# A transformer-like chain on one core: the second MLP's token blocks taken in pairs with Strassen's seven products

## The chip, the cores and the metric

The kernel runs on one core of a Trainium2 chip. The metric is device time of one execution in microseconds (us); lower is better. Engines are named as the profile names them: PE is TensorE (its weight load PEld stands apart), DVE VectorE, ACT ScalarE, POOL GpSimd, SP the queue from which most DMAs are issued.

## The reference

Everything is float32 but the weights, which are float64 (two 32-bit words for each element).

```
attention, per batch and head, 576 tokens x 64:   q' = softmax over features of q, k' = softmax over tokens of k
                                                  x  = q' @ (k'^T @ v)
x reshaped to 4608 tokens x 512 features
first MLP:   h = x @ w_in (512 x 2048);  g = h * clip(h + 3, 0, 6) / 6;  x = g @ w_out (2048 x 512)
second MLP:  h = x @ w_in2;              g = h * sigmoid(h);             out = g @ w_out2
```

## The kernel before

The 4608 tokens are nine blocks of 512 (`BLK`), the 2048 hidden features sixteen tiles of 128 (`NF`). One step is one block and one hidden tile; there are 9 x 16 steps of the first MLP, then 9 x 16 of the second. Every matmul operand is split in two fp32r parts, a rounded upper one and the remainder as lower one, and each product is three matmuls (upper x upper, upper x lower, lower x upper). So a step has 12 matmuls of the first layer (`mm1`, L430: four tiles of 128 input features x 3, 512 tokens as the moving columns) and 12 of the second (`mm2`, L500 and L502). Between them stands the gate (L461 and above): ScalarE's activation, VectorE's product, ScalarE's cast to the upper part, VectorE's subtraction for the lower part. In the first MLP `mm2` leaves its sum with features on partitions, written to `yd` in DRAM (`finish`, L512); in the second one the gate's result is the stationary operand, so the sum has tokens on partitions and is stored as it is.

The order of all instructions on every engine is the order in which the code writes them. The first block is ordered by a small planner (`Plan`); everything after it by the loop at L829. In each step of this loop stand the steps of the attention (a unit is two heads of one block; it takes seven steps, of which `begin` gives the first): among them `k_max` (L227 to L229) at the end of a unit's first step, and in the next one the PE transpose `k_turn` (L234), after `mm1`. In every fourth step of the loop (those with number 1 modulo 4) the next unit's first step meets the older unit's fifth, with the kv scaling `kv_upper` (L291).

The second MLP's weights come as float64. `Conv` turns a tile of 128 x 512 into the two fp32r parts: `begin` (two ScalarE operations), `bits` (three VectorE operations), `upper` (a ScalarE cast), `lower` (a VectorE subtraction). During blocks 1 to 7 of the first MLP, 32 conversions are done, each within one step, and stored to `wd` in DRAM from the single buffer "sp" (L157); the raw tiles are loaded by `load_w`. In the first MLP's last block the converted weights come back with `load_split` into the 16 "wi" and 16 "wo" tiles, where they stay for the second MLP. Its input blocks are read back with `load_y` and split with `split_y`.

PSUM has eight banks of 512 columns: two "h", two "a", four "y0" to "y3". The pools of SBUF that the change uses again are `wts` (16 "wi" and 16 "wo" tiles of 4 KB a partition), `xs` (two of 16 KB), `raw`, `tmp` (six of 2 KB), `gs` and `att`.

## Time and profile before

| what | value |
|---|---|
| three timed runs | 1704.63, 1705.07, 1707.39 us (median 1705.07) |
| profiled execution, first to last instruction (its span) | 1703.8 us |
| its own time around the span | not listed; the median of the timed runs is 1.3 us above the span |
| mean granted clock of TensorE | 0.999 of full speed |
| PE, DVE, ACT, POOL busy | 1669.1, 782.8, 613.6, 77.0 us |
| moved by DMA | 139.22 MB |

The span is that of one execution under the profiler. Busy time counts an engine's instructions, not its waits. Matmuls overlap one another in the list, so the path's cost of one is read from the distance of their starts.

### The profile page before, as it was taken

What the parts mean: (1) busy time and instruction counts of PE and PEld (TensorE: products, weight loads), DVE (VectorE), ACT (ScalarE), POOL (GpSimd) and SP (SyncE); (2) the same over time, 40 slices, a digit from 0 to 9 for tenths busy, and PEclk for the clock granted to TensorE, in tenths of its full rate; (3) what the DMA queues carried; (4) which work ended last, traced back from release to release, by engine and by line L of the source; (5) the groups of instructions that cost most, each with busy time, mean ns of one, the idle gap of its engine ahead of it and who ended that gap; (6) DMA issues with size and microseconds to landing.
All of it is one profiled execution on the core that took longest, in us unless ns stands there. A gap on an engine that the chain in (4) does not pass through costs nothing.

```text
span 1703.8 us, 20315 instructions
## 1 busy us (share of the span) xinstructions
PE 1669.1 (98%) x7868; PEld 1362.7 (80%) x7868; DVE 782.8 (46%) x1424; ACT 613.6 (36%) x1073; POOL 77.0 (5%) x82
## 2 busy tenths in 40 slices
PE   6999999999999999999999999999999999999998
PEld 4777887888788877888888888888888888888887
DVE  8997555565656555555323232223332223332322
ACT  6885344443444344434222222222222222222222
POOL 2110000000000000000000000000000000000000
PEclk9999999999999999999999999999999999999999
DMA  8912443443444335232464010101010101000000
GB/s 259 318 38 83 109 123 105 114 133 108 121 115 133 106 97 139 81 106 62 143 209 153 9 38 13 37 13 38 13 37 13 37 13 36 14 31 20 21 5 25
DMA packets 169808, 139.22 MB, mean 82 GB/s; under 512 B 105840, under 2 KB 140656, under 8 KB 169712
## 3 DMA queue, kind: packets, MB, share of 16 engines
q1 hardware_dynamic: 106752, 122.68, 23.2%
q10 hardware_dynamic: 62960, 15.25, 4.0%
q8 instruction: 62, 1.02, 0.3%
q14 instruction: 34, 0.28, 0.0%
HBM read 95.16 MB, written 42.73 MB: 81 GB/s over the span
## 4 chain that ended last, share of the span: by engine, by line
PE 86%; DVE 7%; ACT 2%; DMA 2%; issue 1%; ACTq 1%; POOL 0%; DVEq 0%; POOLq 0%
PE h L430 41%; PE y L502 23%; PE y L500 18%; PE pa L388 1%; ACTq L361 1%; DVE fa L127 1%; DVE fa L131 1%; PE pa L274 1%; DVE r L450 1%; DMA zd<-qz 1%; DMA qt<-zd 1%; ACT g L458 1%; DVE fa L120 0%; ACT r L443 0%; ACT fa L114 0%
## 5 line engine op out<-in xcount | busy, mean ns | idle before, releaser
L430 PE MATMUL h<-x,wi 128*128 128x512 f32 x3456 | 841.4, 391 | 2.4 <-DVE wi L154 1.0
L430 PEld LDWEIGHTS h<-x,wi 128*128 128x128 f32 x3456 | 644.8, 188 | 139.3 <-DVE wi L154 2.9
L500 PE MATMUL y<-g,wo 128*128 128x512 f32 x1728 | 420.7, 392 | 0.0
L502 PE MATMUL y<-wo,g 128*128 128x512 f32 x1716 | 412.2, 389 | 0.0
L502 PEld LDWEIGHTS y<-wo,g 128*128 128x128 f32 x1716 | 322.1, 188 | 66.9
L500 PEld LDWEIGHTS y<-g,wo 128*128 128x128 f32 x1728 | 320.9, 188 | 68.2 <-ACT g L458 0.4
L454 DVE TENSOR_TENSOR r<-r,h 128x512 f32<-128x512 f32 x144 | 99.0, 688 | 455.5 <-ACT r L445 455.5
L445 ACT ACTIVATE r<-h 128x512 f32<-128x512 f32 x144 | 86.1, 598 | 468.8 <-PE h L430 468.8
L461 DVE TENSOR_TENSOR g<-r,g 128x512 fp32r<-128x512 f32 x272 | 188.4, 693 | 141.6 <-ACT g L458 129.8
L458 ACT CAST g<-r 128x512 fp32r<-128x512 f32 x272 | 169.0, 621 | 222.6 <-DVE r L450 114.0
L450 DVE SCALAR_TENSOR_TENSOR r<-r,h 128x512 f32<-128x512 f32 x128 | 87.8, 686 | 242.2 <-ACT r L443 241.8
L443 ACT ACTIVATE r<-h 128x512 f32<-128x512 f32 x144 | 86.2, 598 | 165.1 <-PE h L430 154.3
L335 POOL TENSOR_TENSOR qe<-qe,qs 128x512 f32<-128x512 f32 x36 | 37.6, 1045 | 355.7 <-DVE qs L330 351.6
L291 ACT ACTIVATE kv<-pa,rs 64x64 fp32r<-64x64 f32 x56 | 17.3, 309 | 98.9 <-DMA qt<-zd 38.5
L313 POOL TENSOR_TENSOR qe<-qraw,qm 128x512 f32<-128x512 f32 x34 | 35.9, 1056 | 365.4 <-DVE qm L305 278.0
L127 DVE CUSTOM_DVE_ANT_0 fa<-fa,fr 128x1024 uint16<-128x1024 uint16 x64 | 46.3, 723 | 7.6 <-ACT fr L116 0.5
L120 DVE TENSOR_SCALAR fa<-fa 128x512 uint32<-128x512 uint32 x64 | 30.0, 468 | 39.0 <-ACT fa L114 38.8
L388 PE MATMUL pa<-qT,kv 128*128 128x512 f32 (+7 forms) x192 | 38.3, 329 | 1.1 <-DVE qT L373 1.1
L264 ACT ACTIVATE ke<-ke 128x640 f32<-128x640 f32 x32 | 23.7, 739 | 40.3 <-DVE ke L254 40.3
L388 PEld LDWEIGHTS pa<-qT,kv 128*128 128x128 f32 x192 | 31.2, 196 | 6.4 <-DVE qT L373 3.2
L398 ACT CAST x<-pa 128x512 fp32r<-128x512 f32 x36 | 21.1, 585 | 29.0 <-PE pa L388 28.9
L274 PEld LDWEIGHTS pa<-vbuf,ke 128*64 128x64 f32 (+1 forms) x560 | 20.8, 136 | 11.7 <-issue 6.7
(96 smaller groups left out, 716.8 us busy)
## 6 DMA issues: line engine op xcount, KB each, us to landing
wd<-sp SPq DMA_DIRECT2D x32, 512.0 KB, 3.0
yd<-o SPq DMA_DIRECT2D x36, 256.0 KB, 2.8
yr<-yd SPq DMA_DIRECT2D x36, 256.0 KB, 2.7
wi_early<-in_moe_w_in_dram SPq DMA_DIRECT2D x16, 512.0 KB, 9.3
wo_early<-in_moe_w_out_dram SPq DMA_DIRECT2D x16, 512.0 KB, 9.5
wi_raw<-in_moe_w_in_dram SPq DMA_DIRECT2D x16, 512.0 KB, 4.9
wo_raw<-in_moe_w_out_dram SPq DMA_DIRECT2D x16, 512.0 KB, 4.7
wi<-wd SPq DMA_DIRECT2D x16, 512.0 KB, 3.6
```

Of the source, the lines that this page charges most:

```text
L127: nc.vector.tensor_tensor(out=au, in0=au, in1=self.r, op=ALU.add)
L274: nc.tensor.matmul(pk[d, 0 : D + 1], t[0:n, j, d], tv[0:n, j, h, :], start=(j == 0), stop=(j == KCH),)
L388: nc.tensor.matmul(pv[:, :, p0 : p0 + n], w[:, a, :], qT[:, c, :, p0 : p0 + n], start=(n_ == 0 and p0 == 0), stop=(n_ == 2), skip_group_ch ...
L430: nc.tensor.matmul(h, w[:, a, c, :], x[:, e, c, :], start=(c == 0 and n == 0), stop=(c == NC - 1 and n == 2),)
L443: nc.scalar.activation(self.r, self.h, AF.Relu, bias=3.0)
L445: nc.scalar.activation(self.r, self.h, AF.Sigmoid)
L450: nc.vector.scalar_tensor_tensor(out=r, in0=r, scalar=6.0, in1=h, op0=ALU.min, op1=ALU.mult)
L454: nc.vector.tensor_tensor(out=r, in0=r, in1=h, op=ALU.mult)
L458: nc.scalar.copy(self.g[:, 0], self.r)
L461: nc.vector.tensor_tensor(out=self.g[:, 1], in0=self.r, in1=f32(self.g[:, 0]), op=ALU.subtract)
L500: nc.tensor.matmul(y[c], w[:, a, cs], g[:, e, :], start=st, stop=sp)
L502: nc.tensor.matmul(y[c], g[:, e, cs], w[:, a, :], start=st, stop=sp)
```

## The change

The second MLP's first eight blocks to be worked on (1 to 8) are taken as four pairs; block 0 follows at the end as before. For a pair (j, j+1), a layer is one product of 2 x 2 blocks: the weights' blocks are `A11`, `A12`, `A21`, `A22` (halves of the inputs by neighbouring hidden tiles in the first layer, with a slot of 256 columns), the tokens' blocks `B11`, `B21` of block j and `B12`, `B22` of block j+1. Seven products replace eight:

```
weights' sums   S1 = A21 + A22   S2 = S1 - A11   S3 = A11 - A21   S4 = A12 - S2
tokens' sums    T1 = B12 - B11   T2 = B22 - T1   T3 = B22 - B12   T4 = B21 - T2
products        P1 = A11 B11   P2 = A12 B21   P3 = S4 B22   P4 = A22 T4   P5 = S1 T1   P6 = S2 T2   P7 = S3 T3
```

Both layers of a pair are done one after the other: for each of eight pairs of hidden tiles (`NPR` = 8) seven `inner` units of 6 matmuls each with the gate of its four results, then 7 x 8 `outer` units of 6 matmuls, product by product. An `outer` unit takes its token operand from `split` (ScalarE cast) and `split_low` (VectorE subtraction), up to three units ahead, through four buffers. The weights' parts lie in DRAM (`ws`, 128 parts of 256 KB, four halves and three sums for each pair of tiles and layer, and the fourth half alone) and are streamed by `fetch`, two parts of 256 KB at a time, through a ring of six buffers, anew for every pair of blocks. The sums of the second layer's products are gathered in eight SBUF rows (`fixed`), transposed in `turn` by PE, and stored.

In the first MLP, blocks 1 to 8, the conversions go by `Parts`: two tiles at once over seven steps (steps 1 to 7 and 8 to 14 of a block): `convert` of one and of the other, `sums` on GpSimd, and four steps with a cast, a subtraction and two stores each. In the first MLP's last block `first_operands` makes the first pair's token operands.

Core of the diff ("..." where lines are left out):

```diff
-    wd = dram.tile([NF, 2, P, 2, DM], F32, name="wd")
+    ws = dram.tile([2, 4 * NF, P, DM], F32, name="ws")
...
+    class Parts:
...
+        def convert(self, n):
+            self.conv[n].begin()
+            self.conv[n].bits()
+        def sums(self):
...
+            self.s = raw.tile([P, 4, HALF], F32, tag="raw", name="ws_sum")
...
+            for to, x, y, op in (
+                ("S1", "A21", "A22", ALU.add), ("S2", "S1", "A11", ALU.subtract),
+                ("S3", "A11", "A21", ALU.subtract), ("S4", "A12", "S2", ALU.subtract),
+            ):
+                nc.gpsimd.tensor_tensor(out=at[to], in0=at[x], in1=at[y], op=op)
+        def upper(self, n):
...
+            self.t = att.tile([P, 2, DM], F32R, tag="sp", bufs=1, name="sp")
+            nc.scalar.copy(self.t[:, 0], self.src)
+        def lower(self, n):
+            t = self.t
+            nc.vector.tensor_tensor(out=t[:, 1], in0=self.src, in1=f32(t[:, 0]), op=ALU.subtract)
+            for h, name in enumerate(self.names[n]):
+                nc.sync.dma_start(
+                    ws[self.o, slot(self.o, self.i, name)].rearrange("p (a d) -> p a d", a=2),
+                    f32(t)[:, :, h * HALF : (h + 1) * HALF],
+                )
...
+    def fetch(k):
+        o, m = divmod(k % (7 * NPR), 7 * NPR // 2)
+        nc.sync.dma_start(
+            f32(ring[k % len(ring)]),
+            ws[o, 2 * m : 2 * m + 2].rearrange("s p d -> p s d"),
+        )
...
+    def raw_x(to, j, h):
+        nc.sync.dma_start(to, yd[j, 2 * h : 2 * h + 2].rearrange("c p n -> p c n"))
+    def x_split(name, src=None):
+        hi, lo = op[name]
+        if src is None:
+            src = f32(lo)
+        nc.scalar.copy(hi, src)
+        nc.vector.tensor_tensor(out=lo, in0=src, in1=f32(hi), op=ALU.subtract)
+    def x_sum(to, x, y, how):
+        nc.gpsimd.tensor_tensor(out=to, in0=x, in1=y, op=how)
+    def x_steps(j):
...
+            t3=lambda: x_sum(st1, low("B22"), st2, ALU.subtract),
+            t1=lambda: x_sum(st2, st2, low("B11"), ALU.subtract),
+            t2=lambda: x_sum(st1, st1, low("B11"), ALU.add),
+            t4=lambda: x_sum(st1, low("B21"), st1, ALU.subtract),
+            T3=lambda: x_split("T3", st1),
...
+    KEYS = ("P1", "P7", "P6", "P5", "P3", "P4", "P2")
...
+        def inner(b, n, p):
...
+            for c in range(2):
+                ws_ = w[:, :, c * P : (c + 1) * P]
+                for m, (a, e) in enumerate(((0, hi), (0, lo), (1, hi))):
+                    nc.tensor.matmul(
+                        to, ws_[:, a], e[:, c],
...
+        def pair_events(b, n, t):
...
+            when(e["P1"] + 0.1, s1)
+            when(e["P6"] + 0.1, u2)
+            when(e["P5"] + 0.1, s5)
+            when(e["P2"] + 0.1, lambda: sig(b, n, "A"))
+            when(e["P2"] + 0.7, lambda: mul(b, n, "A", 0, 0))
+            when(e["P7"] + 0.1, u3)
+            when(e["P7"] + 0.6, c22)
+            when(e["P7"] + 1.1, lambda: sig(b, n, "22"))
+            when(e["P3"] + 0.1, c12)
+            when(e["P7"] + 1.7, lambda: mul(b, n, "22", 1, 1))
...
+            when(e["P3"] + 1.9, t3)
+            when(e["P3"] + 2.0, t1)
+        def split(b, p, i, u):
+            if u % 4 < 2:
+                t = gs.tile([P, 2, BLK], F32R, tag="g", name="gsp")
+            else:
+                tag = "sp" if u % 4 == 2 else "qT"
+                t = att.tile([P, 2, BLK], F32R, tag=tag, bufs=1, name="gsp")
+            d["sp", b, p, i] = t
+            nc.scalar.copy(t[:, 0], source(p, i))
+        def split_low(b, p, i):
+            t = d["sp", b, p, i]
+            add(t[:, 1], source(p, i), f32(t[:, 0]), ALU.subtract)
+            if p == "P1":
+                g1 = g_of(2 * i)
+                add(g1[:, 0], op["spare"][:, i], g1[:, 0], ALU.add, nc.gpsimd)
+            if p == "P6":
+                g1 = g_of(2 * i)
+                add(g1[:, 0], g1[:, 0], g_of(2 * i + 1)[:, 0], ALU.subtract, nc.gpsimd)
+        def outer(b, p, i):
...
+            for m in range(2):
+                for k, (a, e) in enumerate(((0, 0), (0, 1), (1, 0))):
+                    nc.tensor.matmul(
+                        d[b, p][m], w[:, a, m * P : (m + 1) * P], t[:, e],
...
+        def join(b, p):
+            for m in range(2):
+                one, two, three, c22 = fixed[4 * m : 4 * m + 4]
+                if p == "P1":
+                    nc.scalar.copy(one, d[b, p][m])
+                if p == "P6":
+                    add(two, d[b, p][m], one)
+                    add(three, d[b, "P7"][m], two)
+                if p == "P5":
+                    add(c22, d[b, p][m], three)
+                    add(two, d[b, p][m], two)
...
+        def turn(j, k, bank=bank):
...
+                    nc.tensor.transpose(
+                        at[:, c * P : (c + 1) * P], x[:, i * P : (i + 1) * P], ident
+                    )
+            o = small("o2")
+            nc.scalar.copy(o, at)
...
+            nc.sync.dma_start(rows[i], o)
...
+            for u in range(7 * NPR):
+                p, i = KEYS[u // NPR], u % NPR
+                t = start[u]
+                when(t - LOOK + 0.2, lambda b=b, p=p, i=i, u=u: split(b, p, i, u))
+                when(t - LOOK + 0.5, lambda b=b, p=p, i=i: split_low(b, p, i))
+                when(t, lambda b=b, p=p, i=i: outer(b, p, i))
...
+                if i == NPR - 1:
+                    when(t + 1.3, lambda b=b, p=p: join(b, p))
+            j = 1 + 2 * b
+            if b + 1 < BB:
+                do = x_steps(j + 2)
+                base = start[0]
+                for x, name in (
+                    (3.1, "b22"), (3.2, "b11"), (3.3, "b21"), (14.3, "b12"), (17.5, "t3"),
+                    (19.6, "T3"), (19.7, "t1"), (22.6, "t2"), (23.6, "T1"), (26.6, "T2"),
+                    (28.6, "t4"), (31.6, "B11"), (34.6, "T4"), (37.6, "B21"), (40.6, "B22"),
+                ):
+                    when(base + x, do[name])
+                for k in range(2 * NCH):
+                    when(T + 3.95 + 5.0 * k, lambda j=j, k=k: turn(j, k))
+            else:
...
+                for f in range(NF):
+                    when(base + (4.2 + 2.2 * f if f < 14 else 100.0), lambda f=f: load_split(f, 0))
+                for f in range(0, NF, 2):
+                    when(base + 48.3 + 0.5 * f, lambda f=f: load_split(f, 1))
...
+                when(uses[k] + 1.0 - 0.01, lambda k=k: fetch(k + 6))
...
+        parts_at = {}
+        for n in range(2 * NPR):
+            for r in range(7):
+                parts_at[(n // 2 + 1) * NF + 1 + 7 * (n % 2) + r] = (n, r)
...
+        steps = [(0, j, f) for j in range(NB) for f in range(NF)]
```

Of the events of `pair_events`, `s1` and `s5` are ScalarE copies of P1 and P5; `u2`, `u3`, `c12` and `c21` are VectorE additions with one operand in PSUM; `c22` and the product of the same result (`mul` with "22") have both operands in SBUF; `sig` is ScalarE's sigmoid; `t3` and `t1` are GpSimd differences of gate results. Times in `when` are in units of one `inner` or `outer` call; the events are sorted by them and written in that order. Within a pair's second layer, unit u starts at base + u + 1 (from the second unit on).

## Rows read from the trace of the kernel before

**Rows 1.** The page: busy us, share of the span, instructions of each engine.

```profile
PE 1669.1 (98%) x7868; PEld 1362.7 (80%) x7868; DVE 782.8 (46%) x1424; ACT 613.6 (36%) x1073; POOL 77.0 (5%) x82
```

**Rows 2.** The page: chain that ended last, by engine and by line.

```profile
PE 86%; DVE 7%; ACT 2%; DMA 2%; issue 1%; ACTq 1%; POOL 0%; DVEq 0%; POOLq 0%
PE h L430 41%; PE y L502 23%; PE y L500 18%; PE pa L388 1%; ACTq L361 1%; DVE fa L127 1%; DVE fa L131 1%; PE pa L274 1%; DVE r L450 1%; DMA zd<-qz 1%; DMA qt<-zd 1%; ACT g L458 1%; DVE fa L120 0%; ACT r L443 0%; ACT fa L114 0%
```

**Rows 3.** Windows: us, busy PE PEld DVE ACT POOL, PEclk, DMA share, GB/s.

```profile
48.00:72.00 24.00, 23.89 (x121) 18.82 (x122) 23.24 (x46) 20.79 (x39) 2.25 (x2) 1.00 1.06 401
1050.00:1150.00 100.00, 100.00 (x443) 82.81 (x442) 29.05 (x43) 26.04 (x44) 0.00 (x0) 1.00 0.07 22
153.00:704.00 551.00, 542.06 (x2798) 440.39 (x2798) 327.49 (x655) 225.90 (x404) 46.98 (x45) 1.00 0.42 117
704.00:912.50 208.50, 208.29 (x936) 171.66 (x935) 89.00 (x148) 69.57 (x121) 9.39 (x9) 1.00 0.40 129
```

**Rows 4.** Timeline in the second MLP: start, us, engine, line, operation, count.

```profile
1301.71 2.88 PE L502 MATMUL y<-wo,g 128*128 128x512 f32 x12
...
1307.15 2.88 PE L502 MATMUL y<-wo,g 128*128 128x512 f32 x12
```

**Rows 5.** Timeline of PE around five transposes in the first MLP.

```profile
147.48 0.27 PE L246 MATMUL pa<-ident,mx 128*128 128x128 f32 x1
147.59 0.60 PE L343 MATMUL pa<-ident,qe 128*128 128x128 f32 x4
147.95 3.00 PE L430 MATMUL h<-x,wi 128*128 128x512 f32 x12
150.79 2.88 PE L500 MATMUL y<-g,wo 128*128 128x512 f32 x12
```

**Rows 6.** Groups by line: out<-in, shapes, count, busy us, mean ns, idle before.

```profile
L461 DVE TENSOR_TENSOR g<-r,g 128x512 fp32r<-128x512 f32 x272 | 188.4, 693 | 141.6 <-ACT g L458 129.8 <-PE y L502 5.5 <-PE y L500 1.4
L458 ACT CAST g<-r 128x512 fp32r<-128x512 f32 x272 | 169.0, 621 | 222.6 <-DVE r L450 114.0 <-DVE r L454 108.6
L335 POOL TENSOR_TENSOR qe<-qe,qs 128x512 f32<-128x512 f32 x36 | 37.6, 1045 | 355.7 <-DVE qs L330 351.6 <-ACT x L398 4.1
L254 DVE TENSOR_TENSOR ke<-kbuf,pa 128x640 f32<-128x640 f32 x28 | 22.8, 814 | 2.0 <-PE pa L246 2.0
```

**Rows 7.** PE's waits (sum, times, longest) from 153 us; timeline around two k_turns.

```profile
PE pa L234 <- DVE m L229: 8.2, 7, 1.4
...
254.14 0.63 ACT L291 ACTIVATE kv<-pa,rs 64x64 fp32r<-64x64 f32 x2 [2.89 <-DMA qt<-zd]
...
260.76 0.29 DVE L229 TENSOR_TENSOR m<-m,kbuf 128x128 f32<-128x128 f32 x1
261.19 0.30 PE L234 MATMUL pa<-ident,m 128*128 128x128 f32 x1 [1.37 <-DVE m L229]
...
305.83 0.63 ACT L291 ACTIVATE kv<-pa,rs 64x64 fp32r<-64x64 f32 x2 [4.00 <-PE h L430]
...
309.89 0.29 DVE L229 TENSOR_TENSOR m<-m,kbuf 128x128 f32<-128x128 f32 x1
310.58 0.27 PE L234 MATMUL pa<-ident,m 128*128 128x128 f32 x1
```

**Rows 8.** DMA issues: out<-in, queue, count, KB each, median us to landing.

```profile
wi<-wd SPq DMA_DIRECT2D x16, 512.0 KB, 3.6
```

**Rows 9.** Timeline of DVE and POOL where they meet, in the first block.

```profile
59.30 1.05 POOL L335 TENSOR_TENSOR qe<-qe,qs 128x512 f32<-128x512 f32 x1 [13.26 <-DVE qs L330]
59.36 0.69 DVE L467 SCALAR_TENSOR_TENSOR h<-r,h 128x512 f32<-128x512 f32 x1
...
60.82 0.68 DVE L154 TENSOR_TENSOR wo<-fa,wo 128x512 fp32r<-128x512 f32 x1
61.42 0.68 DVE L127 CUSTOM_DVE_ANT_0 fa<-fa,fr 128x1024 uint16<-128x1024 uint16 x1
61.79 1.21 POOL L313 TENSOR_TENSOR qe<-qraw,qm 128x512 f32<-128x512 f32 x1 [1.45 <-PE pa L343]
62.13 1.42 DVE L131 SCALAR_TENSOR_TENSOR fa<-wi_early,fa 128x512 uint32<-128x512 uint32 x1
```

More of the change, by code (lines that the diff above doesn't have):

```diff
@@ L880, in efficient_attention_then_two_mlps @@
                 q_norm(here[2], nc.gpsimd)
[L881 to L889 removed]
+            job, r = parts_at.get(n, (None, None))
+            if r in (0, 1):
+                made[job].convert(r)
+                if r == 1 and job + 1 < 2 * NPR:
+                    load_w(1, 2 * made[job + 1].i, made[job + 1].o)
+            if r == 2:
+                made[job].sums()
             mm1(s)
@@ L911, in efficient_attention_then_two_mlps @@
                 q_store(here[3])
-            for c in convs:
-                c.upper()
-                c.lower()
+            if r is not None and r >= 3:
+                made[job].upper(r - 3)
+                made[job].lower(r - 3)
             if 2 in has_k:
```

295 lines of the change are left out of this document (259 added, 36 removed), and 3 rows, old and new, of the table new.

## The prediction

> **What bounds the kernel now.** I read the page's busy shares first: TensorE works 98% of the 1703.8 us span, no other engine half of it [rows 1]. The chain of waits says the same of the path: 86% of it is TensorE, and its three largest parts are the two MLPs' matmuls [rows 2]. Then the stages: from 1050 to 1150 us TensorE is busy without a gap at granted clock 1.00, VectorE 29%, ScalarE 26%, GpSimd not at all, and the DMA engines move 22 GB/s; between 153 and 704 us, with the attention beside the first MLP, TensorE is idle 9 us in 551 and VectorE busy 59% [rows 3]. The timeline gives the second MLP's pace: from one second-layer group of 12 matmuls to the next is 1307.15 - 1301.71 = 5.44 us, and 24 matmuls lie in it, so one 128x512 matmul costs 0.2267 us on the path (its listed 0.39 us overlaps its neighbours) [rows 4]. In this stage only fewer matmuls shorten the time, as long as the rest keeps pace.
>
> **The change, part by part.** The sum starts from the profiled span, 1703.8 us; the median of the timed runs is 1705.07, so 1.3 us is added at the end.
>
> *Matmuls removed.* Two blocks of the second MLP are 2 x 16 steps x 24 = 768 matmuls. In the change a pair has 7 products x 8 indices x 6 matmuls = 336 per layer, 672 in all. Four pairs save 4 x 96 = 384, and 384 x 0.2267 = 87.0 us. The ninth block and the tail stay as they are.
>
> *Transposes added.* The second layer now leaves its sum with features on partitions, so each pair needs 8 turns of four 128x128 fp32 transposes, 128 in all. Between the matmuls of the first MLP five such transposes took: first issue 147.48, next group 147.95, and that group's 12 matmuls end 2.84 instead of 2.72 us later (150.79); 0.59 us for five, 0.118 each [rows 5]. 128 x 0.118 = 15.1 us on the path. Their evictions and stores lie on ScalarE and SP, beside.
>
> The Trainium skill, page "TensorE: Matmul & The Clock Gate", section "Part 4: PE-mode transpose", gives about 0.275 us for a 128x128 transpose inside a kernel and says that transposes do not count like matmuls for the clock. By that figure the term would be 35.2 us and the sum 20 us later; the rows time the same operation, at granted clock 1.00, so they are used.
>
> *First MLP.* 32 more casts (0.62 us) and 32 more subtractions (0.69 us) [rows 6] are 20 us of ScalarE and 22 us of VectorE over eight blocks, 64 half-width sums go to GpSimd, and 128 stores of 256 KB replace 32 of 512 KB. These engines have room [rows 3]. What counts is the one wait that TensorE has here: k_turn waits for the last k_max operation, 7 times, 8.2 us [rows 7]. It comes when a conversion falls in the step of k_max: without one, k_max ended 4.35 us after the kv scaling began (305.83 to 310.18) and TensorE did not wait; with a whole one it ended 6.91 us after (254.14 to 261.05) and TensorE waited 1.37 [rows 7]. So a conversion delays it 2.56 us, and some 1.2 of it is covered. Now the first half of a conversion (two ScalarE operations, three VectorE operations; the second half's 0.69 gone, so 1.9 us) falls into two of the four such steps of a block: 12 steps at 1.9 less a cover of 0.4 to 1.2 us are 8 to 18 us, against 8.2 now. I take a middle, 12, so +4 us; ends 0 and +20 (the upper one if the single "sp" buffer, whose store must land before the next cast, makes ScalarE wait as well, and with it all VectorE work queued behind the subtraction). The operands of the first pair are made in the last block, whose VectorE is 43% busy [rows 3]; nothing for it.
>
> *Weights from DRAM.* 56 fetches of 512 KB per pair, each for two units of 6 matmuls (2.72 us): 193 GB/s. Each waits on SP for the last matmul of its slot's old contents; behind it queue the next fetches, the raw x loads and the output stores. It is issued ten units, 13.6 us, before its use, and a 512 KB load lands in 3.6 us [rows 8]. The stage from 48 to 72 us moved 401 GB/s [rows 3]. In the last pair's second layer the ninth block's weights come beside it (14 x 512 KB in 41 us, 179 GB/s): 372, still below. Nothing on the path.
>
> *First layer of a pair.* Per index n (42 matmuls, 9.52 us): 9 VectorE operations, 6.2 us, 6 ScalarE, 3.6, two GpSimd, 2.1 [rows 6]. Each combination has three or more units before TensorE writes over its bank. Nothing, as estimate; the upper end is a rival.
>
> *Second layer of a pair.* Here each unit (1.36 us) needs a fresh split: a ScalarE cast and a VectorE subtraction of two SBUF operands. GpSimd adds 8 sums of 512 columns during P1, 8 during P6, and in the first three pairs four of 1024 columns (t1 to t4) for the next pair's x. What matters is whether GpSimd and VectorE can work at the same time. At 61.79 a GpSimd operation starts; the VectorE operation with two SBUF operands that starts at 62.13 takes 1.42 instead of 0.69 us and ends 0.55 after GpSimd's (63.55 to 63.00). A VectorE operation that reads PSUM, at 59.36 beside GpSimd's 59.30, is not delayed, and free VectorE operations follow each other every 0.60 us (60.82, 61.42) [rows 9]. So in these phases a sum (1.05) and a subtraction (0.60) go one after the other: 1.65 us per unit against TensorE's 1.36.
>
> The Trainium skill, page "SBUF — State Buffer", section "SBUF: two separate sides", says that the pair of ports shared by the two engines is held for a whole instruction and the other engine fully blocks. The rows agree for single meetings; with both queues full no run here shows it.
>
> A 1024-column split is 512's plus 512 columns at about 1.0 ns (640 columns 0.814, 512 0.693 [rows 6]): 1.2 us; a 1024-column sum, twice 1.05 less its start, 2.0. The three stretches of a full pair:
> - P1, from its second split to the eleventh unit: 10 subtractions 6.0, two first-layer operations with two SBUF operands 1.2, 9 sums 9.45, half of four PSUM-reading operations 1.3: 18.0 us, against 11.5 units, 15.6. About 2.0 late, less where they overlap better.
> - P6 to P5, 13 splits: 7.8; 8 sums 8.4; t3, t1, t2 6.0; splits T3 and T1 2.4; joining P6 with four VectorE operations 2.6: 27.2 us. TensorE takes 14.4 units, 19.6, counted from the earliest time that four split buffers allow. 7.6 late.
> - P5 with the B11 split and four joins before the backlog is gone: 1.0.
>
> That is 10.6 us for a full pair, three of them, 31.8. The last pair has no t sums, only four 512-column splits of y: 4 us. Together 36 us of new TensorE waits, whose releaser is the subtraction in split_low. Ends: 10 us if the ports do not exclude each other (joins and wide splits alone), 50 if GpSimd wins each tie, so that T1 and T2 come later still.
>
> **Sum.** 1703.8 - 87.0 + 15.1 + 4 + 36 = 1671.9, plus 1.3: **1673 us**.
>
> **Rivals.**
> - *The exclusion costs little.* VectorE and GpSimd interleave, or GpSimd falls behind harmlessly (the P6 sums are needed only in P4). For it: the first MLP's GpSimd work delays hardly anything. Against it: the meetings of [rows 9], and T1 waits in line behind those sums. Second-layer waits 10: 1673 - 26 = 1647 us.
> - *The first layer doesn't keep pace.* VectorE runs 9 operations per n in written order, four of them behind a ScalarE sigmoid; if each n adds 1 us of TensorE wait, 32 x 1 = 32: 1705 us, no change. Against it: 6.2 us of work in 9.5 and three units of lead. For it: today VectorE's chain has idle time in front of almost every operation.
> - *Slower: the weight stream sets the pace.* Break-even is a fetch period of 2.72 + (87.0 - 15.1 - 4)/224 = 3.02 us (173 GB/s) if nothing else waits. If one fetch must land before the next makes headway, its 3.6 us [rows 8] is the period: 224 x 0.88 = 197 us of waits, about 1705 - 68 + 197 = 1834. For it: 2 KB rows, one queue, all behind in-order waits. Against it: six buffers, and 401 GB/s with 512 KB loads in the same queue.
>
> **How the numbers follow.** Forecast 60%, little exclusion 22%, first layer 10%, stream 8%. Forecast's own spread with the first-MLP ends: 1652 to 1700. The range leaves out the stream, the upper half of the first-layer case and the lowest outcomes: 1640 to 1699. This kernel's runs tell 0.2%, 3.4 us, from no change. Faster: 60 + 22 + half of the first-layer case, with a little taken off for it: 87%; same 3%; slower 10%.
>
> **What would show it.** About 384 fewer 128x512 matmuls in the groups by line and 128 more transposes near 0.1 us apart. In the windows of a pair's second layer, TensorE idle 8 to 12 us of some 88, and in its waits the matmul of outer on VectorE's split_low subtraction, gathered at P6; almost none in the first layer. VectorE subtractions of 1.2 us and more beside GpSimd. In the first MLP k_turn's wait for k_max near 12 us. DMA near 200 GB/s in the second MLP, with no matmul waiting for it. The forecast is wrong if the waits are spread evenly over both layers, if a DMA is their releaser, or if TensorE runs without a gap in P6.

## The result, and the profile after

The changed kernel took 1725.15 us (median of 4 runs, 1723.13 to 1726.64) against 1704.99: a ratio of 1.0116 [1.0101, 1.0130], slower by 20 us. The forecast was 1673 us, its range 1640 to 1699, with a chance of 10% for slower. All times that follow are against the kernel before on the same chip.

The page of the changed kernel, busy time and chain, in the columns of [rows 1, 2]:

```profile
span 1721.3 us, 21607 instructions
PE 1631.2 (95%) x7612; PEld 1312.2 (76%) x7612; DVE 1080.8 (63%) x1748; ACT 741.7 (43%) x1285; POOL 357.4 (21%) x290
PE 70%; DVE 17%; ACT 4%; DMA 4%; issue 2%; POOL 1%; ACTq 1%; SPq 0%; DVEq 0%; POOLq 0%
```

TensorE has 256 instructions fewer (384 matmuls less, 128 transposes more, as forecast), but it falls from 98 to 95% busy, and VectorE's share of the chain rises from 7 to 17%. Where the time is lost shows in two views. First the windows of the changed kernel (columns as in [rows 3]): two of the first MLP, two of pairs of the second:

```profile
153.00:704.00 551.00, 519.11 (x2631) 420.58 (x2630) 319.76 (x626) 217.50 (x390) 78.11 (x86) 0.98 0.43 122
704.00:956.00 252.00, 243.68 (x1101) 200.20 (x1100) 128.58 (x212) 97.44 (x167) 37.91 (x36) 0.99 0.35 109
956.00:1037.00 81.00, 81.00 (x359) 67.11 (x358) 50.65 (x76) 33.20 (x56) 21.07 (x16) 1.00 0.61 213
1037.08:1206.49 169.41, 160.53 (x706) 128.18 (x705) 120.71 (x150) 73.25 (x122) 58.15 (x36) 1.00 0.59 199
1375.89:1545.29 169.40, 162.74 (x706) 130.16 (x705) 120.68 (x150) 73.14 (x122) 58.11 (x36) 0.98 0.59 199
```

Between 153 and 704 us, where TensorE was idle 9 us before [rows 3], it is idle 32. The first layer of the first pair (956 to 1037) runs without a gap. A pair takes 169.40 us; by the matmul pace of [rows 4] it should take 2 x 7 x 8 x 1.36 = 152.3, and 156.1 with the 32 transposes. So 13.3 us are lost in each of the three full pairs (the window goes from one pair's second layer to the next one's).

The waits of TensorE in the changed kernel (sum, times, longest):

```profile
PE pa L296 <- DVE m L291: 37.1, 11, 5.9
PE pb L1089 <- DVE gsp L978: 20.9, 16, 2.3
PE pb L1089 <- ACT gsp L1070: 2.7, 3, 0.9
PE y L562 <- ACT g L520: 2.4, 1, 2.4
```

L296 is k_turn, L291 the last operation of k_max (L234 and L229 of [rows 7]); L1089 is the second layer's matmul in outer, L978 the helper that issues every addition, here split_low's subtraction; L562 is the first MLP's second layer. The second MLP now begins at 956.8 us instead of 912.8: the first MLP lost 44 us, and the second won 26.5 (912.8 to the span's end before, 791.0; 956.8 to the end after, 764.5).

### The first loss, in the first MLP

Of the 11 waits of k_turn six take 5.3 to 5.9 us and five about 0.8. The timeline of the changed kernel ahead of one long wait:

```profile
200.91 0.37 SPq L97 DMA_DIRECT2D wi_raw<-in_moe_w_in_dram  x1
201.49 0.33 ACTq L417 DMA_DIRECT2D zd<-qz  x1
206.11 2.67 ACTq L423 DMA_DIRECT2D qt<-zd  x4
208.88 0.63 ACT L353 ACTIVATE kv<-pa,rs 64x64 fp32r<-64x64 f32 x2 [6.78 <-DMA qt<-zd]
209.54 0.66 ACT L114 ACTIVATE fa<-wi_raw 128x512 f32<-128x512 f32 x1
...
213.50 0.93 DVE L523 TENSOR_TENSOR g<-r,g 128x512 fp32r<-128x512 f32 x1 [0.19 <-ACT g L520]
213.85 1.17 POOL L196 TENSOR_TENSOR ws_sum<-fa 128x256 f32<-128x256 f32 x1
214.35 0.94 DVE L289 TENSOR_TENSOR m<-kbuf 128x256 f32<-128x256 f32 x1
...
216.06 0.29 DVE L291 TENSOR_TENSOR m<-m,kbuf 128x128 f32<-128x128 f32 x1
216.50 0.44 PE L296 MATMUL pa<-ident,m 128*128 128x128 f32 x1 [5.50 <-DVE m L291]
```

Three things come together. The reload of the normalised queries (L423) waits on ScalarE's queue for its own store (L417) to land; that takes 4.62 us here (4.4 to 5.1 in the six steps with a long wait), and 2.0 to 2.1 us in the other steps up to 790 us. At 826 us, in the last block, it takes 5.1 us once more, and TensorE waits the 2.4 us of L562. Ahead of the store, by 0.58 us, stands a 512 KB raw load on SP's queue. ScalarE computes nothing meanwhile (6.78 us). Then the conversion (L114 and what follows) goes before the step's own work, which is what the prediction had. Then the new sums of weight parts on GpSimd (L196) run beside VectorE's subtraction and maximum: 0.93 us instead of 0.69, 0.94 instead of 0.42.

With each long wait comes a stretch at half clock: six of them in the clock records of the trace, 3.4 or 6.8 us each, 34.1 us in all. They begin 0.2 to 2.3 us before the wait ends, so 6.9 us of them lie in the waits and 27.2 behind. The windows of the changed kernel ahead of the wait and right behind it:

```profile
156.50:216.50 60.00, 54.50 (x278) 44.35 (x277) 36.37 (x71) 23.50 (x43) 10.93 (x13) 1.00 0.45 126
216.50:220.00 3.50, 3.50 (x10) 2.78 (x11) 3.03 (x7) 1.15 (x2) 0.17 (x1) 0.54 0.03 7
```

The granted clock is 1.00 (2.4 GHz) up to the wait and 0.54, so mostly 1.2 GHz, behind it; 10 matmuls begin in 3.5 us where 15 would. All waits of this stretch are 40.2 us (37.1, 2.4 and one of 0.7), where the kernel before had 9.0: 31.2 more, 28.9 of them k_turn's. At half clock matmuls start 0.427 us apart (216.9 to 219.6 us) instead of 0.227, so about half of the 27.2 us, 13.6, is lost on top: 44.8 us by this account, where 44.1 are missing.

### The second loss, in the second layer of a pair

The groups by line of the changed kernel (columns as in [rows 6]):

```profile
L978 DVE TENSOR_TENSOR gsp<-g,gsp 128x512 fp32r<-128x512 f32 x192 | 178.8, 957 | 40.9 <-ACT gsp L1070 40.5
L978 POOL TENSOR_TENSOR g<-spare,g 128x512 f32<-128x512 f32 x32 | 51.1, 1614 | 19.5 <-DVE gsp L978 19.5
L978 POOL TENSOR_TENSOR g<-g,g 128x512 f32<-128x512 f32 x32 | 50.8, 1602 | 31.9 <-DVE gsp L978 31.9
L978 POOL TENSOR_TENSOR spare<-g,g 128x512 f32<-128x512 f32 x32 | 43.2, 1351 | 352.0 <-DVE g L978 315.2 <-PE pb L991 36.8
L900 DVE TENSOR_TENSOR xo<-spare,xo 128x1024 fp32r<-128x1024 f32 x16 | 26.1, 1630 | 11.0 <-ACT xo L899 11.0
L903 POOL TENSOR_TENSOR spare<-spare,xo 128x1024 f32<-128x1024 f32 x8 | 21.7, 2718 | 17.6 <-DVE xo L900 15.1 <-DMA xo<-yd 2.5
```

VectorE's subtraction of two SBUF operands takes 0.957 us in the mean (0.693 in [rows 6]); GpSimd's sums for P1 and P6, beside it, 1.61 and 1.60, and those of the first layer 1.35. The timelines of VectorE, GpSimd and TensorE in P6 of the changed kernel show how they hold each other up:

```profile
1069.42 7.94 DVE L978 TENSOR_TENSOR gsp<-g,gsp 128x512 fp32r<-128x512 f32 x4
...
1073.38 3.42 POOL L978 TENSOR_TENSOR g<-g,g 128x512 f32<-128x512 f32 x2
1076.77 2.83 POOL L903 TENSOR_TENSOR spare<-spare,xo 128x1024 f32<-128x1024 f32 x1
1077.28 3.41 DVE L900 TENSOR_TENSOR xo<-spare,xo 128x1024 fp32r<-128x1024 f32 x1
1080.61 0.68 DVE L978 TENSOR_TENSOR gsp<-g,gsp 128x512 fp32r<-128x512 f32 x1
1081.35 1.66 PE L1089 MATMUL pb<-gsp,ring 128*128 128x512 f32 x6 [2.27 <-DVE gsp L978]
```

The wide split begins at 1077.28, 0.51 us into GpSimd's wide sum, and ends 1.09 us behind it (1080.69 to 1079.60): 3.41 us instead of 1.22. The subtraction queued behind it is the one that TensorE waits 2.27 us for.

The weights' stream is no part of it. The DMA issues of the changed kernel:

```profile
ring<-ws SPq DMA_DIRECT2D x224, 512.0 KB, 3.7
...
wi_raw<-in_moe_w_in_dram SPq DMA_DIRECT2D x16, 512.0 KB, 4.4
wo_raw<-in_moe_w_out_dram SPq DMA_DIRECT2D x16, 512.0 KB, 4.1
...
zd<-qz ACTq DMA_DIRECT2D x27, 256.0 KB, 2.0
```

No matmul waited for a ring load, with 199 GB/s in the pairs' windows. The last three rows belong to the first loss: a raw load lands in 4.1 to 4.4 us, the store of the queries in 2.0 at the median.

### The profile page after: what moved, and what is told of

It reads as the page before. It is cut to its first block, busy times and chain, and to the rows that moved or that the text cites. A ratio compares the mean times of both kernels' runs of the same rounds, so it can differ in the third digit from the quotient of the medians.

```text
span 1721.3 us, 21607 instructions
## 1 busy us (share of the span) xinstructions
PE 1631.2 (95%) x7612; PEld 1312.2 (76%) x7612; DVE 1080.8 (63%) x1748; ACT 741.7 (43%) x1285; POOL 357.4 (21%) x290
## 4 chain that ended last, share of the span: by engine, by line
PE 70%; DVE 17%; ACT 4%; DMA 4%; issue 2%; POOL 1%; ACTq 1%; SPq 0%; DVEq 0%; POOLq 0%
PE h L492 19%; PE y L562 17%; PE pb L991 17%; PE pb L1089 11%; DVE gsp L978 5%; PE y L564 2%; DMA zd<-qz 2%; DVE fa L127 2%; PE pa L450 1%; DVE fa L131 1%; DMA qt<-zd 1%; DVE r L512 1%; DVE xo L900 1%; ACTq L423 1%; DVE g L523 1%
## 5 line engine op out<-in xcount | busy, mean ns | idle before, releaser
L492 PE MATMUL h<-x,wi 128*128 128x512 f32 x1920 | 472.6, 393 | 2.3 <-DVE wi L152 1.0
L562 PE MATMUL y<-g,wo 128*128 128x512 f32 x1728 | 432.6, 400 | 2.4 <-ACT g L520 2.4
L492 PEld LDWEIGHTS h<-x,wi 128*128 128x128 f32 x1920 | 356.6, 188 | 79.3 <-DVE wi L152 2.8
L562 PEld LDWEIGHTS y<-g,wo 128*128 128x128 f32 x1728 | 329.6, 193 | 73.4 <-ACT g L520 2.8
L1089 PE MATMUL pb<-gsp,ring 128*128 128x512 f32 x1344 | 326.2, 399 | 24.8 <-DVE gsp L978 20.9
L1089 PEld LDWEIGHTS pb<-gsp,ring 128*128 128x128 f32 x1344 | 251.8, 190 | 97.9 <-DVE gsp L978 43.3
L991 PE MATMUL pb<-xo,ring 128*128 128x512 f32 x1344 | 313.3, 391 | 0.0
L991 PEld LDWEIGHTS pb<-xo,ring 128*128 128x128 f32 x1344 | 250.5, 188 | 51.7
L978 DVE TENSOR_TENSOR gsp<-g,gsp 128x512 fp32r<-128x512 f32 x192 | 178.8, 957 | 40.9 <-ACT gsp L1070 40.5
L1070 ACT CAST gsp<-g 128x512 fp32r<-128x512 f32 x192 | 117.0, 620 | 108.2 <-PE pb L1089 74.3
L505 ACT ACTIVATE r<-h 128x512 f32<-128x512 f32 x144 | 85.9, 597 | 169.7 <-PE h L492 164.6
L523 DVE TENSOR_TENSOR g<-r,g 128x512 fp32r<-128x512 f32 x144 | 103.1, 716 | 53.4 <-ACT g L520 43.8
L978 POOL TENSOR_TENSOR spare<-g,g 128x512 f32<-128x512 f32 x32 | 43.2, 1351 | 352.0 <-DVE g L978 315.2
L978 DVE TENSOR_TENSOR g<-r,pb 128x512 f32<-128x512 f32 x96 | 65.9, 686 | 70.8 <-ACT r L1004 70.4
L978 DVE TENSOR_TENSOR U<-pb,s 128x512 f32<-128x512 f32 x64 | 44.2, 691 | 24.1 <-PE pb L991 22.3
```

The costliest lines, as they stand in the source:

```text
L492: nc.tensor.matmul(h, w[:, a, c, :], x[:, e, c, :], start=(c == 0 and n == 0), stop=(c == NC - 1 and n == 2),)
L505: nc.scalar.activation(self.r, self.h, AF.Relu, bias=3.0)
L523: nc.vector.tensor_tensor(out=self.g[:, 1], in0=self.r, in1=f32(self.g[:, 0]), op=ALU.subtract)
L562: nc.tensor.matmul(y[c], w[:, a, cs], g[:, e, :], start=st, stop=sp)
L978: (eng or nc.vector).tensor_tensor(out=out, in0=a, in1=b, op=how)
L991: nc.tensor.matmul(to, ws_[:, a], e[:, c], start=p in ("P1", "P6", "P5") and c == 0 and m == 0, stop=c == 1 and m == 2, skip_group_check=True,
```

## The experiments

The kernel before and the changed one differ by two losses with different places, so the runs come in three groups: which of the two is how large, what the first is made of, what the second is made of. Each run changes the changed kernel unless its diff says otherwise.

### Which part costs what

**e1_parts_moved**: the jobs that make weight parts begin one or two steps later, so that no conversion falls in a step of k_max.

```
-  parts_at[(n // 2 + 1) * NF + 1 + 7 * (n % 2) + r] = (n, r)
+  parts_at[min(18 + 8 * n, 137) + r] = (n, r)
```

> Only the steps of the weights' conversion jobs in the first MLP are moved: they start at steps 18, 26, 34, ... (the last at 137) instead of 17, 24, 33, 40, ..., so that no job's second conversion and its GpSimd sums stand in a step in which k_max ends. Theory (collision in the step of k_max, then half clock after the long gap): k_turn's wait for k_max falls from 37.1 us to under 10, no stretch at half clock between 153 and 704 us, the second MLP starts near 917 us instead of 957, time about 1685 us. Rival (the added stores and loads as such delay the attention's zd store and q_load, wherever the conversions stand): the wait stays above 25 us and the time above 1708.

Measured: 1689.42 us, 0.9907 [0.9893, 0.9922], 36 us below the changed kernel. The second MLP begins at 922.5. One stretch at half clock, 3.4 us, is left, where none was expected. The wait for k_max is gone; a smaller one, of the same kind, stands in its place:

```profile
PE pa L450 <- DVE qT L435: 16.6, 13, 2.3
```

The conversion now falls in the steps where VectorE makes the lower half of the queries, which TensorE needs next.

**e5_parts_step3**: the jobs begin one step later still, past both.

```
+  parts_at[(19 + 8 * n if n < 14 else 32 + 7 * n) + r] = (n, r)
```

> Only the start of the conversion jobs differs from the changed kernel: steps 19, 27, ..., 123, 130, 137, so the two conversions stand in steps 3 and 0 modulo 4, away from the steps in which k_max (1) and the x matmul's operand (2) are due. Theory (collision by position): neither k_turn nor the x matmul waits over 1 us, no half clock between 153 and 704 us, second MLP from about 915 us (957 in the changed kernel, 922 with the jobs from step 18), time 1681 to 1684. Rival (the added work binds wherever it stands): one or the other wait comes back, time 1689 or more.

Measured: 1670.11 us, 0.9792 [0.9777, 0.9806], below the 1681 to 1684 expected. There is no wait for k_max, no half clock in the first MLP, and the second MLP begins at 899.9, not 956.8. With the same work, only placed otherwise, the whole of the first loss is gone, and the second MLP begins 13 us earlier than in the kernel before; 9.0 of them are that kernel's own waits in this stretch, the rest is not resolved.

**e7_no_layer_sums**: the outer sums on GpSimd (those of P1 and P6 and t1 to t4) left out.

> From the changed kernel the 16 GpSimd sums of each pair's second layer and t1 to t4 are left out (the products then read operands without these sums); casts, subtractions, joins and all matmuls stay. Theory (the exclusion): of the 13.3 us per pair 10 to 12 go, time 1685 to 1692. Rival (joins and wide splits in bunches are the main part): at least 6 us per pair stay, time above 1697.

Measured: 1680.19 us, 0.9852 [0.9835, 0.9868], 45 us below the changed kernel and somewhat below the 1685 to 1692 expected; a pair takes 156.3 us, and TensorE waits for nothing in the second MLP. VectorE's subtraction (L982 in this run) is back near its own price:

```profile
L982 DVE TENSOR_TENSOR gsp<-g,gsp 128x512 fp32r<-128x512 f32 x192 | 132.4, 709 | 55.0 <-ACT gsp L1074 55.0
```

So all of the 13.3 us per pair but 0.2 come with these sums, and the transposes and the matmuls cost what was forecast: 156.1.

### What the first loss is made of

**e4_no_part_sums**: the four sums of weight parts per job left out.

```
-  nc.gpsimd.tensor_tensor(out=at[to], in0=at[x], in1=at[y], op=op)
+  pass
```

> The four GpSimd sums of the weights' parts are left out (S1 to S4 hold the two halves of the second tile instead); the conversions, casts, subtractions and stores stay where they are. Theory (in the step of the long waits the sums hold VectorE off by 1.2 us, the conversion itself by 1.9, and ScalarE's late start by 2.8): the six long waits of k_turn go from 5.5 to about 4.3 us, time 8 to 12 us shorter, about 1715. Rival (the sums' exclusion is the main part): waits of about 1.4 us, as before the change, and no half clock: 1680 to 1690.

Measured: 1716.79 us, 1.0067 [1.0051, 1.0084], as expected. The k_turn waits fall from 37.1 to 31.0 us, half clock from 34.1 to 27.3; the sums are the smallest of the three parts.

**e8_all_in_kmax_step**: every job's second conversion in a step of k_max, to see whether the long waits become 11.

```
+  parts_at[min(16 + 8 * n, 136) + r] = (n, r)
```

> The conversion jobs start at steps 16, 24, 32, ..., 136, so that every job, not each second one, has its second conversion and its sums in a step in which k_max ends. Theory (collision by position): 12 long waits of k_turn of about 5.5 us instead of 6, and as many stretches at half clock, time 1755 to 1775. Rival (one long wait per block has another cause, such as the raw load or the block's end): 6 long waits, time within 10 us of 1725.

Measured: 1726.77 us, 1.0126 [1.0105, 1.0146]. The expectation missed; what was measured is the rival's six long waits within 10 us of 1725. The waits stay split, six of about 4.6 us and five of about 2.4 (39.4 in all). In the six the store of the queries takes 4.1 to 4.4 us to its reload, in the five 2.0 to 2.1. Conversion and sums stand in all eleven (in the step of the wait at 269 us k_max's first operation takes 0.94 us, as in the changed kernel). So the conversion with its sums makes the shorter wait, and the late store goes with the longer one.

**e9_raw_load_later** and **e11_raw_load_after_store** looked for what makes the store late: each job's second raw load one step later, and the same load put on ScalarE's queue.

```
-  if r == 6 and job + 1 < 2 * NPR:
-      load_w(1, 2 * made[job + 1].i + 1, made[job + 1].o)
+  if r == 0 and job > 0:
+      load_w(1, 2 * made[job].i + 1, made[job].o)            # e9
+      load_w(1, 2 * made[job].i + 1, made[job].o, nc.scalar) # e11
```

> From the changed kernel only the place of one DMA is changed: the next job's second raw tile (512 KB) is loaded at the end of that job's first step instead of the end of the job before, so it no longer goes out 0.6 us ahead of the attention's zd store. Theory (three parts of about 1.9, 1.2 and 2.5 us make the 5.5 us wait of k_turn: the conversion, the GpSimd sums, and a zd store that lands after 4.6 instead of 2.0 us, for which ScalarE's next loads wait with the conversion and the gate behind them): zd store to the loads that read it 2.0 to 2.2 us everywhere, the six long waits 2.5 to 3.2 us, less half clock, time 1700 to 1710. Rival (the store is late through the added ws stores or vbuf loads): no change, 1721 to 1728.

> From the changed kernel only the load of each next job's second raw tile is changed: it is issued from ScalarE's queue at the end of the job's first step, behind the attention's zd store in that queue, so it can't go out ahead of it. Theory (the raw load just ahead of the store makes the store land late, and ScalarE's next loads, the conversion and the gate wait for that): zd store to the loads that read it about 2.0 us also in the six steps (4.4 to 5.1 in the changed kernel), the six long waits of k_turn 2.4 to 3.4 us instead of 5.5, time 1698 to 1712. Rival (something else delays the store there, such as the vbuf loads): the delay stays over 4 us, time 1720 or more.

Measured: 1731.85 us, 1.0159 [1.0144, 1.0174], and 1755.00 us, 1.0291 [1.0276, 1.0307]. Both expectations missed, and both runs moved the wrong load. In e9 the store took 5.6 to 6.0 us in five of the six steps, where two raw loads now stand ahead of it, by 2.1 and 0.57 us; in e11 it took 4.1 to 4.5, about as in the changed kernel. e11 also gave TensorE 24.1 us of waits for the queries' lower half: on ScalarE's queue the moved load goes out late (in one step at 264.95 us, landing at 270.23), and the conversion that reads it starts at 270.33, ahead of that step's work. The load 0.58 us ahead of the store is the next job's first one, issued as soon as the running job's first conversion frees the buffer.

**e13_first_raw_load_later**: that load moved behind the sums, one step later.

```
   if r in (0, 1):
       made[job].convert(r)
-      if r == 1 and job + 1 < 2 * NPR:
-          load_w(1, 2 * made[job + 1].i, made[job + 1].o)
   if r == 2:
       made[job].sums()
+      if job + 1 < 2 * NPR:
+          load_w(1, 2 * made[job + 1].i, made[job + 1].o)
```

> From the changed kernel only the next job's FIRST raw tile is loaded one step later (after the sums are written, not after the second conversion). Its load went out as soon as the first conversion had freed the buffer, 0.6 us ahead of the zd store; the two trials before moved the other load and left this one there. Theory (conversion 1.9, sums 1.2, late zd store 2.5 us make the 5.5 us wait): zd store to the loads that read it 2.0 to 2.4 us everywhere, the six long waits of k_turn 2.4 to 3.4 us, time 1698 to 1712. Rival (the store is late through the vbuf loads or the ws stores): 4 us or more remain, time above 1719.

Measured: 1704.75 us, 0.9997 [0.9987, 1.0006], 20 us below the changed kernel. The same step in the timeline of this run:

```profile
200.60 0.33 ACTq L417 DMA_DIRECT2D zd<-qz  x1
202.96 2.85 ACTq L423 DMA_DIRECT2D qt<-zd  x4
...
213.53 0.45 PE L296 MATMUL pa<-ident,m 128*128 128x128 f32 x1 [3.43 <-DVE m L291]
```

The reload follows its store by 2.36 us (2.0 to 3.3 in the six steps, where 2.0 to 2.4 was expected), and the wait is 3.43 us instead of 5.50 (2.9 to 4.1 in the six).

**e14_and_no_part_sums**: e13 without the sums of e4.

> The same with the four GpSimd sums of the parts left out as well (S1 to S4 hold the second tile's halves). Theory: only the conversion's own delay stays in the step of k_max: its six waits 1.2 to 2.2 us, no half clock between 153 and 704 us or nearly none, time 4 to 10 us below the run without this second edit. Rival (once the store is in time the sums no longer matter): within 3 us of that run.

Measured: 1691.47 us, 0.9923 [0.9906, 0.9939], 13 us below e13, somewhat past the 4 to 10 expected. TensorE's waits for k_max in this run (L189 is a one-column fill of 0.06 us that keeps the sums' tile, right behind k_max on VectorE; it stands in for k_max as what the wait is put down to):

```profile
PE pa L293 <- DVE ws_sum L189: 13.8, 6, 3.0
PE pa L293 <- DVE m L288: 4.0, 5, 0.8
```

Together the runs make one account. For each kernel: all waits of TensorE from 153 us to the second MLP; the half clock there that lies outside these waits, from the clock records of the trace; the change in the first plus half the change in the second; and the begin of the second MLP, both against the changed kernel (us):

| kernel | waits | half clock outside them | worked out | measured |
|---|---|---|---|---|
| changed | 40.2 | 27.2 | | 956.8 |
| before | 9.0 | 0 | -44.8 | -44.1 |
| e10 (below) | 4.2 | 0 | -49.6 | -50.0 |
| e1 | 16.6 | 3.4 | -35.5 | -34.4 |
| e4 | 34.4 | 23.2 | -7.8 | -8.3 |
| e8 | 40.5 | 34.5 | +3.9 | +2.9 |
| e9 | 49.6 | 24.2 | +7.9 | +7.7 |
| e11 | 61.6 | 44.4 | +29.9 | +29.7 |
| e13 | 25.6 | 19.2 | -18.6 | -19.3 |
| e14 | 18.9 | 6.8 | -31.5 | -31.6 |
| e5 | 0 | 0 | -53.8 | -56.9 |

All rows but the last agree within 1.1 us; the 3.1 us of e5 are not resolved. In e2, e3 and e7, whose steps of the first MLP are those of the changed kernel, the second MLP begins at 957.9 to 959.9: executions differ by up to 3 us here, so a difference of that size tells nothing by itself.

So k_turn's 37.1 us of waits have three parts: the store held up by the load ahead of it, 12.4 us (37.1 to 24.7 in e13); the sums beside VectorE, 6.9 (to 17.8 in e14); and what the conversions in the steps of k_max make, the 17.8 that are left. Of these the five short waits are 4.0 and the six others 13.8; why the six stay longer was not separated. The half clock adds half of its length outside the waits, 13.6 us.

**e10_before_moved**: the kernel before, with its 32 conversions in steps with the numbers 3 and 0 modulo 4, as e5 has them.

```
-  spills.setdefault(first + n * (last - first) // (2 * NF), []).append(n)
+  spills[sorted([19 + 4 * i for i in range(28)] + [32, 64, 88, 112])[n]] = [n]
```

> The kernel before, with only its 32 conversions moved: to steps 19, 23, ..., 127 and 32, 64, 88, 112, so none stands in a step in which k_max ends. Theory (part of what the moved jobs give is not Strassen's: the first MLP of the kernel with jobs from step 19 ends 13 us before that of the kernel before): k_turn's waits of 8.2 us go, time 1692 to 1698. Rival (the gain in the first MLP came from spreading the conversion over more steps): 1702 to 1706.

Measured: 1698.55 us, 0.9965 [0.9952, 0.9977], just above the 1692 to 1698 expected; k_turn's wait falls from 8.2 us to 2.1, and another grows from 0.8 to 2.1. So the place of conversions was worth 6 us before the change and 55 us (e5) after it.

### What the second loss is made of

**e2_sums_on_vector**: the outer sums on VectorE, at the same places.

```
-  nc.gpsimd.tensor_tensor(out=to, in0=x, in1=y, op=how)
+  nc.vector.tensor_tensor(out=to, in0=x, in1=y, op=how)
...
-  add(g1[:, 0], op["spare"][:, i], g1[:, 0], ALU.add, nc.gpsimd)
+  add(g1[:, 0], op["spare"][:, i], g1[:, 0], ALU.add)
```

(and the P6 sum likewise)

> Only the engine of the second layer's 16 sums and of t1 to t4 is changed, from GpSimd to VectorE. Theory (GpSimd and a VectorE operation with two SBUF operands exclude each other, so a GpSimd sum costs VectorE 1.3 to 2.8 us and a VectorE one only 0.6 to 1.2): the 13.3 us that a pair's second layer takes beyond its matmuls fall to 3 to 5, time about 1695 us although VectorE gets 14 us more work per pair. Rival (VectorE is simply overloaded there): the second layer gets longer, 1735 us or more.

Measured: 1706.40 us, 1.0009 [0.9999, 1.0018]. A pair loses 7.3 us instead of 13.3, more than the 3 to 5 expected: without GpSimd in the way, the work still bunches in P1 and at P6.

**e3_p6_sums_late**: the sums that P4 needs moved out of P6, the wide sums and splits brought forward.

```
-  if p == "P6":
-      add(g1[:, 0], g1[:, 0], g_of(2 * i + 1)[:, 0], ALU.subtract, nc.gpsimd)
+  for i in range(NPR):
+      when(start[0] + 25.0 + 1.6 * i, lambda i=i: for_p4(i))
```

> Only the order is changed: the eight GpSimd sums of P6, which P4 needs, are written from unit 25 on, 1.6 units apart, instead of beside P6's splits, and b12, t3, T3, t1, t2, T1, T2, t4 come 3 to 5 units earlier. The same work on the same engines. Theory (it is the meeting of GpSimd and VectorE in P6 that costs): 13.3 us per pair fall to 4 to 6, time about 1698 us. Rival (the sum of the work over the whole second layer is what binds): the waits move to P5 and P3, time within 6 us of 1725.

Measured: 1715.19 us, 1.0054 [1.0039, 1.0069]. A pair loses 10.5 us; the waits moved to other units (17, 18 and 27 to 31) more than they went. The expected 1698 was missed.

**e6_both**: e5, with the sums on VectorE and spread over the layer: those of P1 from 7.6 units on at 0.9 units each, those for P4 from 35.0 on, and the wide sums and splits between them.

```
-  (3.1, "b22"), ..., (14.3, "b12"), (17.5, "t3"), (19.6, "T3"), (19.7, "t1"), (22.6, "t2"), ...
+  (3.1, "b22"), ..., (11.5, "b12"), (16.0, "t3"), (17.6, "T3"), (19.6, "t1"), (21.6, "T1"), ...
+  when(start[0] + 7.6 + 0.9 * i, lambda i=i: for_p6(i))
+  when(start[0] + 35.0 + 0.9 * i, lambda i=i: for_p4(i))
```

> The jobs as from step 19, and in the second layer all 16 sums and t1 to t4 on VectorE, written one by one in the products that have room: P6's operand sums during P7, P4's during P3, t3, t1, t2, t4 and the seven splits from unit 16 to 53. Theory (the second layer has enough VectorE time if GpSimd never holds it off and nothing comes in bunches: 38.6 + 13.4 + 9.6 + 9.1 = 71 of 77.6 us): TensorE waits 1 to 3 us per pair instead of 13.3, time 1640 to 1650. Rival (VectorE at 91% makes the splits late anyway): 5 us or more per pair, above 1655.

Measured: **1625.62 us, 0.9531 [0.9517, 0.9545]**, below the 1640 to 1650 expected: it beats both kernels. Its page and its windows (a stretch of the first MLP and one pair):

```profile
PE 1593.0 (98%) x7612; PEld 1302.5 (80%) x7612; DVE 1064.9 (66%) x1828; ACT 741.5 (46%) x1285; POOL 216.1 (13%) x210
153.00:704.00 551.00, 551.00 (x2849) 450.86 (x2844) 344.93 (x678) 236.43 (x424) 84.67 (x91) 1.00 0.46 131
1060.00:1216.27 156.27, 156.27 (x706) 129.25 (x705) 115.69 (x170) 73.12 (x121) 21.35 (x16) 1.00 0.63 216
```

TensorE has no gap in either stretch, at granted clock 1.00. VectorE does more operations than in the changed kernel (1828 instead of 1748) in less busy time (1064.9 us instead of 1080.8), since the subtraction and the wide split are back at their own price:

```profile
L978 DVE TENSOR_TENSOR gsp<-g,gsp 128x512 fp32r<-128x512 f32 x192 | 132.6, 707 | 22.9 <-ACT gsp L1070 22.8
L900 DVE TENSOR_TENSOR xo<-spare,xo 128x1024 fp32r<-128x1024 f32 x16 | 19.8, 1237 | 3.1 <-ACT xo L899 3.1
```

**e12_spread_on_gpsimd**: e6 with the sums back on GpSimd at the spread places.

> The fastest version so far (jobs from step 19, the second layer's sums spread out), with the 16 sums and t1 to t4 back on GpSimd at the same places. Theory (GpSimd and VectorE take turns, so these sums hold VectorE off for 16 x 1.29 + 4 x 2.8 = 32 us in a second layer where it has 57 us of its own work and 77.6 us of time): 6 to 12 us per pair come back, time 1648 to 1665. Rival (the places alone made the difference): 1624 to 1630.

Measured: 1663.51 us, 0.9753 [0.9737, 0.9770], as expected; a pair takes 167.4 us. TensorE waits for the subtraction again, and the groups show its price back:

```profile
PE pb L1091 <- DVE gsp L978: 19.9, 15, 2.2
```

```profile
L978 DVE TENSOR_TENSOR gsp<-g,gsp 128x512 fp32r<-128x512 f32 x192 | 184.5, 988 | 34.0 <-ACT gsp L1070 34.0
L978 POOL TENSOR_TENSOR g<-spare,g 128x512 f32<-128x512 f32 x32 | 54.6, 1740 | 0.0
```

Loss per full pair, in us, by engine and place of the outer sums:

| | places of the change | spread |
|---|---|---|
| GpSimd | 13.3 (changed kernel) | 11.3 (e12) |
| VectorE | 7.3 (e2) | 0.2 (e6) |

Neither step alone does it: spreading is worth 2.0 us with GpSimd and 7.1 with VectorE. Where the two engines hold each other up, moving so many sums to better places gave little; without that, their places were the rest of the loss.

## Why the prediction was wrong

**The step that failed is the first MLP's term: +4 us forecast, ends 0 and +20; measured +44.** The mechanism named, the half conversion that delays k_max and so k_turn, was right, and the term was mis-sized. The conversions left 17.8 us of waits with store and sums out of the way (e14), where 12 were taken: the cover, whose upper end of 1.2 us the prediction read off one case of [rows 7], is there in the five short waits (0.8 us, 1.9 less 1.1) and not in the other six (2.3 in the mean). The sums of weight parts, put down as work on an engine with room, add 6.9, since they delay VectorE's operations in the very step. And the queue crossing was not looked at: the prediction counted the conversion's engine time but not that its buffer, once free, lets the next raw load go out right ahead of a store that ScalarE waits for; 12.4 us more. The other suspect it named for the upper end, the single "sp" buffer, took next to no part: ScalarE waits once for its store, 0.7 us. What it left out altogether is the clock: in [rows 3] the granted clock is 1.00 throughout, and the waits of [rows 7] are at most 1.4 us; with the waits of 5.3 us and more came stretches at the half level, 13.6 us on top of the waits. With the measured 44 in this term alone the forecast would have been 1713 us, outside its range; with the second layer's 45 alone, 1682.

**The second layer: +36 forecast, 45 measured** (764.5 us against 791.0 - 87.0 + 15.1 = 719.1). Place, releaser and engine were as said: e7 shows that the loss comes with the sums, and e12 against e6 that at the same places it hangs on GpSimd doing them. For a full pair the sum was 2.0 + 7.6 + 1.0 = 10.6 against 13.3. In the gaps between the matmuls the first and the last stretch came out at 2.1 and 1.0; the middle one, P6 to P5, took 9.9 where 7.6 were forecast. There the wide sums were priced by twice a row of GpSimd with a broadcast operand (1.05 us, [rows 6]), 2.0 us; they took 2.72 in the mean. The 512-column sums of two full operands take 1.29 us where nothing meets them (at 1008.19 us, in the first layer), not 1.05. At these prices its sum would be some 4 us more (8 x 0.24 and 3 x 0.72), 11.7 late, so about 2 us overlapped that it had counted one after the other. The last pair lost about 5.5 us where 4 were forecast.

The Trainium skill, page "SBUF — State Buffer", section "SBUF: two separate sides", says that a VectorE operation with two SBUF inputs and a GpSimd operation that reads SBUF lock each other out for a whole instruction. The meeting at 1077 us agrees: 3.41 us for the split instead of 1.22, its end 1.09 us behind GpSimd's.

**What held.** Matmuls removed, -87.0, and transposes, +15.1: with the sums left out a pair took 156.3 us against 156.1 worked out. The 0.275 us of the Trainium skill's page "TensorE: Matmul & The Clock Gate", section "Part 4: PE-mode transpose", is near the 0.27 us that the list gives for one transpose [rows 5]; as an estimate of the path's cost it would have made 8.8 us of a pair's 32 transposes instead of 3.8, and the pair 161. The distance of the starts, 0.118 us, was nearer. The weights' stream (no wait, 199 GB/s, 3.7 us to landing) and the first layer (no gap) cost nothing, as said. With 44.0 and 45.4 for 4 and 36 the sum is 1721.3 us, the span; as both are differences of spans, this is no check of its own, and the 156.3 us of e7 is.

**The rivals.** The side "slower" came true by none of the mechanisms named for it: neither the stream nor the first layer. It took the first MLP, whose own upper end of +20 lay within the forecast's case and should have been a rival with its own price. The forecast's own spread, 1652 to 1700, also doesn't follow from the ends given: with both terms at their ends, 0 and 10 or +20 and 50, the sum is 1643 or 1703, and the result lies outside of either. "The exclusion costs little" is refuted by the 45 us of e7.

**The change by itself.** Against e10, the kernel before with its conversions placed as well, e6 is 1625.62 - 1698.55 = -73 us; matmuls and transposes alone make -87.0 + 15.1 = -71.9. That the two agree so well is in part luck: by the traces the second MLP is 69.3 us shorter (791.1 to 721.8), and the first 7.0, of which 4.2 are waits of e10. The gain was there, and the changed kernel gave it back in two places.

## What to carry to other kernels

When work is added to a stage whose bound engine is near 100%, list for each step of its schedule what is late next, and price the added work in that step with the loads and stores that move with it, not as a share of an engine's idle time. A wait of the bound engine can cost more than its own length when the clock falls with it (here 13.6 us on top of 40.2), so waits of several us are to be priced at more than they last. Before sums go to GpSimd beside a VectorE that works on SBUF operands, add both engines' times in that stretch as if they were one engine; if the sum doesn't fit, VectorE alone, with the sums spread out, may (e6).

## What the runs showed of the hardware that was not expected

A 512 KB load issued on SP's queue 0.58 us ahead of a 256 KB store on ScalarE's made the store's landing 4.4 to 5.0 us instead of 2.0, six times in six; with the load elsewhere it was 2.0 to 3.2 (e13). In five of the six the store landed 0.7 to 0.8 us behind the load. The Trainium skill, page "DMA: Bandwidth & Descriptors", section "Queues, rings and completion order", says that a completion is signalled only after every earlier write of the same DMA engine, across its queues. The trace agrees in those five; in the sixth (the store at 410.61 us) the store landed 0.7 us before the load, so it did not wait for all of it. No run here separates such an order from the two sharing bandwidth.

Half clock did not follow every wait. Behind the six long ones of the changed kernel (5.3 to 5.9 us) it came each time, behind the six of 1.8 to 3.0 us in e14 twice, both times behind one of 2.25 us and not behind the longest two (2.6 and 3.0): the length of the wait alone does not tell it. In the second layer of pairs 2 and 3 of the changed kernel it came too, and the pair took the same 169.40 us as pair 1, whose granted clock was 1.00: there VectorE and GpSimd set the pace, as e7 shows for their sums.
